# Attention and two feed-forward layers on one core: score, read and S matmuls of a batch gathered into two steps instead of three

## The chip, the cores and the metric

The kernel runs on one core of one Trainium2 chip. The metric is the device time of one execution in microseconds (us), from the profiler's clock; before the change three executions took 1313.85, 1314.18 and 1314.67 us.

## The reference, cut to what matters

For each of 8 batches and 8 heads an attention with 32 state rows is computed in both directions, and the joined output (4,608 tokens of 512 numbers) goes through two feed-forward layers with squared ReLU, 512 to 2,048 to 512.

```
scores = scale * x @ state.T ; a = softmax(scores) ; xread = a @ state
scores2 = scale * state @ x.T ; a2 = softmax(scores2) ; sread = a2 @ x
x = concat([xread, sread], axis=2) as (B * S, H * D)
h = max(x @ w_in, 0) ; x = (s * h * h + b) @ w_out          # first layer
h = max(x @ w_in2, 0) ; out = (h * h) @ w_out2              # second layer
```

## The kernel before, in words

Numbers are float32. Most matmuls run on a fast 32-bit format, with every operand split into a high and a low part (`hi`, `lo`), so that one product takes three matmuls.

**Steps.** The first layer is a loop over steps i. A step belongs to one batch j (512 tokens) and one block f of 128 hidden units, 16 steps for a batch. Batches 0 and 1 share steps 0 to 31, batch 2 has steps 32 to 47, batch 3 has 48 to 63, and so on; the last 16 steps are for the 256 state rows of all batches. A step issues 6 matmuls `h` (`mm1`), the ReLU, square and copy on ScalarE (ACT), a subtraction on VectorE (DVE, `low`), and the 12 matmuls `acc` (`mm2`) of the step two before. When a batch's 16 blocks are summed, `evac` takes the four accumulators out: two on DVE, two on ACT, into tiles `ot`, which are stored.

**What rides between the steps.** While batch j runs, the attention of batch b = j + 1 is made ready by jobs that `at_step(step, job, rank)` hangs on the steps. `base` is the first step of the batch that runs meanwhile. Those with matmuls are: `att_sc`, the scores `sc` (16 matmuls, copied out by ACT into the tile `sc`); `att_tp`, 8 transposes `tp` of the softmax (copied by ACT into `a2T`); `att_sr`, the reads `sr` (64 small matmuls), which `att_scale` multiplies on DVE; `att_put`, a transpose `st` of the scaled reads; and `s_mm` for each quarter q of the hidden units, which makes S, the product of the state and `w_in`. One S has 16 matmuls into two PSUM banks, two ACT copies (`S`, the high parts, in `s_parts`), and two DVE subtractions in `s_rest`, which read the same two banks again for the low parts. Scores and S use a quarter-width, half-height piece of the array (64*32 in the rows), reads 128*32, everything else the whole array.

**Order.** The program sets the order by hand; each engine runs its instructions in the order in which the jobs are called, by step and inside a step by rank. On ACT and DVE the same steps carry the preparation of the second layer's weights, one `sums_job` for each of 16 blocks with 15 operations: two loads, `magnitude` on ACT (tile `v`), `bound` and `shift`, `sign` and `low_bits` on DVE (two instructions each), four additions, four `hi` copies on ACT and four `lo` subtractions on DVE. The table `SUMS_AT` gives each operation its step; inside a step they have ranks 8 to 9, so they come behind the attention's jobs.

**Banks.** Every PSUM tile but the accumulators comes from `pst`, which takes four banks in turn (`psa`, `psb`, `psc`, `psc`). So the tile made four calls later sits in the same bank, and its first matmul waits until the last reader of the earlier tile is done.

**`behind`.** On a step listed in `behind`, the 12 `acc` matmuls of the following step are issued at once, behind the step's jobs, and only then the job itself, here `s_rest`:

```
for _, _, fn in sorted(side.pop(i, [])):
    fn()
if i in behind:
    rest_of(i - 1)
    behind.pop(i)()
```

Of the kernel before, what the change touches and what calls it, by code (L numbers as in the profile page):

```python
# [27 lines left out]
F32 = mybir.dt.float32  # L28
# [12 lines left out]
P = 128  # L41
# [47 lines left out]
def attn_mlp2(ctx: ExitStack, tc: tile.TileContext, xT, xn, st, w_in1, w_out1, w_in2, w_out2, s_in, b_in, out):  # L89
# [285 lines left out]
    def s_rest(b, q):  # L375
        t = S_t[b, q]
        for r in range(2):
            nc.vector.tensor_tensor(
                out=t[:, 1, r, :], in0=S_ps.pop((b, q, r)), in1=t[:, 0, r, :].bitcast(F32), op=ALU.subtract
            )  # L380
# [63 lines left out]
    xa = {}  # L444
    sb_t = {}

    def st_load(b):
        sb = sm.tile([P, 2, KD, NS], F32, tag="st", name=f"st{b}")
        nc.sync.dma_start(out=sb, in_=st[b])
        sb_t[b] = sb  # L450

    def att_load(b):
        t = x8([P, KD, S], f"xT{b}", F32)
        kk = KD // 2 if b < 2 else KD
        for k in range(0, KD, kk):
            nc.sync.dma_start(
                out=t[:, k : k + kk, :], in_=xT[b, k * P : (k + kk) * P].rearrange("(k p) s -> p k s", p=P)
            )
        xa[b] = [t, None]

    def att_load_n(b):
        n = x8([P, S // P, DM], f"xn{b}", F32)
        nc.sync.dma_start(out=n, in_=xn[b].rearrange("(t p) d -> p t d", p=P))
        xa[b][1] = n
# [132 lines left out]
    def att_scale(b):  # L597
        srp = srp_t.pop(b)
        s2 = parts2.pop(b)
        pool, tag = (an1, "an") if b else (op, "o")  # L600
        t = pool.tile([P, P], F32, tag=tag, name="srs").rearrange("p (r d) -> p r d", r=2)
        srp_t[b] = t
        for r in range(2):
            src, by = srp[:, r * D : (r + 1) * D], s2[:, r : r + 1]
            if b < 2:
                nc.scalar.activation(out=t[:, r], in_=src, func=ACTF.Copy, scale=by)
            else:
                nc.vector.tensor_scalar(out=t[:, r], in0=src, scalar1=by, scalar2=None, op0=ALU.mult)

    def att_put(b):  # L610
        t = srp_t.pop(b)
        pt = pst(f"st{b}")[:, :P]
        nc.tensor.transpose(out=pt, in_=t.rearrange("p r d -> p (r d)"), identity=ident)
        dst, src = sraw[:, :, b * NS : (b + 1) * NS], pt.rearrange("p (k n) -> p k n", k=KD)
        copy = lambda: nc.scalar.activation(out=dst, in_=src, func=ACTF.Copy)
        return copy if b == 0 else copy()
# [567 lines left out]
    def at_step(i, fn, rank=5):  # L1184

        side.setdefault(i, []).append((rank, len(side.get(i, ())), fn))
# [5 lines left out]
    def step(j, f):  # L1192
        return place[j, 0] + f

    calm = ((att_sc, 5, 0), (att_max, 6, 5), (att_exp, 8, 5), (att_sum, 9, 5), (att_mul, 10, 5), (att_tp, 13, 0),
            (att_sr, 17, 0), (att_scale, 17, 2))
    behind = {}
    for b in range(1, B):
        base = step(2, 0) + (b - 3) * NF if b > 1 else 0
        if b > 1:  # L1200
            at_step(base + 1 + (b == 2), lambda b=b: st_load(b), 6)
            at_step(base + 1, lambda b=b: att_load(b), 6)
            at_step(base + (4 if b > 2 else 1), lambda b=b: att_load_n(b), 6)
            for fn, k, r in calm:
                at_step(base + k, lambda fn=fn, b=b: fn(b), r)
            for c in range(2):
                n = base + 11 + c
                at_step(n, lambda b=b, c=c: att_turn(b, c), 3)
                at_step(n, lambda b=b, c=c: turned.pop((b, c))(), 6)
            at_step(base + (21 if b < B - 1 else 18), lambda b=b: att_put(b), -1)  # L1210
            if b == 2:
                for q in range(NQ):
                    k = base + 4 * q + 5
                    at_step(k, lambda b=b, q=q: s_mm(b, q), 1)
                    at_step(k + (q == 0), lambda b=b, q=q: s_rest(b, q), 0.2 if q == 0 else 9.8)
                continue
            for q, (k, r) in enumerate(((5, 1), (13, 1), (17, 1), (17, 2.5))):
                at_step(base + k, lambda b=b, q=q: s_mm(b, q), r)
            for q in range(2):
                at_step(base + 5 + 8 * q, lambda b=b, q=q: s_rest(b, q), 9.8)  # L1220
            behind[base + 17] = lambda b=b: s_rest(b, 2)
            at_step(base + 18, lambda b=b: s_rest(b, 3), 0.2)
            continue
        for q, n in ((1, 12), (2, 16), (3, 23)):
            at_step(n, lambda b=b, q=q: s_mm(b, q), 1)
            at_step(n + 1, lambda b=b, q=q: s_rest(b, q), 0.2)
# [338 lines left out]
```

## Time and profile before

| what | before |
|---|---|
| median of three executions | 1314.18 us (1313.85 to 1314.67) |
| the profiled execution | 1313.79 us, of which the span of instructions is 1312.0 us |
| TensorE (PE) busy | 1304.6 us, 99% of the span |
| PE weight loads, DVE, ACT busy | 1117.6, 921.6, 805.7 us |
| granted TensorE clock, mean | 1.000 of full speed |

The span runs from the first to the last instruction. PE is the engine that is always at work; the other engines have spare time, which costs nothing as long as PE needn't wait for them. Matmuls overlap, so the time that one costs is read from the start of one row to the start of the next, not from its own length.

### The profile page before, as it was taken

What the parts mean: (1) busy time and instruction counts of PE and PEld (TensorE: products, weight loads), DVE (VectorE), ACT (ScalarE), POOL (GpSimd) and SP (SyncE); (2) the same over time, 40 slices, a digit from 0 to 9 for tenths busy, and PEclk for the clock granted to TensorE, in tenths of its full rate; (3) what the DMA queues carried; (4) which work ended last, traced back from release to release, by engine and by line L of the source; (5) the groups of instructions that cost most, each with busy time, mean ns of one, the idle gap of its engine ahead of it and who ended that gap; (6) DMA issues with size and microseconds to landing.
All of it is one profiled execution on the core that took longest, in us unless ns stands there. A gap on an engine that the chain in (4) does not pass through costs nothing.

```text
span 1312.0 us, 21131 instructions
## 1 busy us (share of the span) xinstructions
PE 1304.6 (99%) x7455; PEld 1117.6 (85%) x7455; DVE 921.6 (70%) x1612; ACT 805.7 (61%) x1482; POOL 0.7 (0%) x7
## 2 busy tenths in 40 slices
PE   8999999999999999999999999999999999999998
PEld 6777777777787878789988888888899999999998
DVE  8998998676676767555456578666776776677665
ACT  6876756676666666766655465445554655565554
POOL 0000000000000000000000000000000000000000
PEclk9999999999999999999999999999999999999999
DMA  8467343443726273440576587665887798788775
GB/s 297 151 229 270 125 151 126 154 147 118 225 89 213 80 243 107 145 153 33 173 212 177 170 265 208 200 179 169 260 265 226 230 323 253 230 278 290 239 224 167
DMA packets 159560, 255.68 MB, mean 195 GB/s; under 512 B 14816, under 2 KB 67040, under 8 KB 159200
## 3 DMA queue, kind: packets, MB, share of 16 engines
q1 hardware_dynamic: 159456, 254.34, 61.3%
q8 instruction: 60, 0.98, 0.3%
q14 instruction: 44, 0.36, 0.1%
HBM read 202.90 MB, written 51.38 MB: 194 GB/s over the span
## 4 chain that ended last, share of the span: by engine, by line
PE 95%; DVE 4%; issue 0%; DMA 0%; ACT 0%; SPq 0%; DVEq 0%
PE acc L691 27%; PE m L923 25%; PE p L947 25%; PE h L642 14%; PE S L353 2%; PE sr L588 1%; PE sc L353 0%; DVE V L172 0%; DMA i1r<-w_in 0%; PE tp L574 0%; DVE g L674 0%; DVE v L172 0%; DVE V L179 0%; DVE o1l L227 0%; DVE V L158 0%
## 5 line engine op out<-in xcount | busy, mean ns | idle before, releaser
L923 PE MATMUL m<-bigx,bigr 128*128 128x384 f32 (+1 forms) x1680 | 366.9, 356 | 0.0
L691 PE MATMUL acc<-g,o1h 128*128 128x512 f32 (+1 forms) x1152 | 341.1, 378 | 0.1
L923 PEld LDWEIGHTS m<-bigx,bigr 128*128 128x128 f32 x1680 | 302.7, 188 | 26.4
L691 PEld LDWEIGHTS acc<-g,o1h 128*128 128x128 f32 x1152 | 211.8, 188 | 45.4 <-issue 3.4
L691 PE MATMUL acc<-g,o1l 128*128 128x512 f32 (+1 forms) x576 | 217.4, 378 | 0.0
L642 PE MATMUL h<-aT,S 128*128 128x512 f32 x768 | 196.9, 393 | 0.0
L947 PE MATMUL p<-g,bigr 128*128 128x384 f32 (+1 forms) x864 | 191.0, 356 | 0.0
L674 DVE TENSOR_TENSOR g<-r,g 128x512 fp32r<-128x512 f32 (+1 forms) x143 | 93.9, 657 | 132.5 <-ACT g L663 132.0
L642 PEld LDWEIGHTS h<-aT,S 128*128 128x128 f32 x768 | 142.2, 188 | 45.3 <-ACT a2T L575 5.0
L947 PEld LDWEIGHTS p<-g,bigr 128*128 128x128 f32 x864 | 155.9, 188 | 13.1
L657 ACT ACTIVATE r<-h 128x512 f32<-128x512 f32 (+1 forms) x143 | 81.7, 571 | 118.1 <-PE h L642 115.5
L750 ACT ACTIVATE sc<-sc 128x384 f32<-128x384 f32 (+1 forms) x120 | 67.9, 566 | 101.3 <-DVE sc L753 100.0
L947 PE MATMUL p<-bigg,bigr 128*128 128x384 f32 (+1 forms) x576 | 129.7, 357 | 0.0
L691 PEld LDWEIGHTS acc<-g,o1l 128*128 128x128 f32 x576 | 108.4, 188 | 20.2
L947 PEld LDWEIGHTS p<-bigg,bigr 128*128 128x128 f32 x576 | 104.1, 188 | 8.9
L750 ACT ACTIVATE v<-m 128x384 f32<-128x384 f32 (+1 forms) x80 | 42.8, 535 | 95.1 <-PE m L923 94.6
L753 DVE TENSOR_TENSOR v<-m,r 128x384 f32<-128x384 f32 (+1 forms) x40 | 24.5, 611 | 106.7 <-PE m L923 106.7
L660 ACT ACTIVATE r<-r 128x512 f32<-128x512 f32 (+1 forms) x143 | 87.1, 609 | 4.5
L663 ACT ACTIVATE g<-r 128x512 fp32r<-128x512 f32 (+1 forms) x143 | 87.0, 608 | 4.5
L753 DVE TENSOR_TENSOR g<-bigt,g 128x384 fp32r<-128x384 f32 (+1 forms) x71 | 41.9, 604 | 16.4 <-ACT g L750 16.3
L753 DVE TENSOR_TENSOR r<-m,v 128x384 f32<-128x384 f32 (+1 forms) x40 | 24.4, 611 | 35.0 <-PE m L923 31.8
L750 ACT ACTIVATE t<-t 128x384 f32<-128x384 f32 (+1 forms) x80 | 45.2, 565 | 1.3
(173 smaller groups left out, 1550.7 us busy)
## 6 DMA issues: line engine op xcount, KB each, us to landing
bigr<-wi SPq DMA_DIRECT2D x280, 256.0 KB, 3.2
bigr<-wo SPq DMA_DIRECT2D x240, 256.0 KB, 3.3
i1r<-w_in SPq DMA_DIRECT2D x16, 512.0 KB, 4.4
xn<-xn SPq DMA_DIRECT2D x8, 1024.0 KB, 9.2
o1r<-w_out SPq DMA_DIRECT2D x16, 512.0 KB, 5.4
x<-ot SPq DMA_DIRECT2D x32, 256.0 KB, 2.7
i2r<-w_in SPq DMA_DIRECT2D x32, 256.0 KB, 4.4
o2r<-w_out SPq DMA_DIRECT2D x16, 512.0 KB, 4.3
```

The costliest lines, as they stand in the source:

```text
L353: nc.tensor.matmul(out=outs[r][k * NS : (k + 1) * NS], lhsT=state[rows, r, k, :], rhs=moving(rows, k), start=True, stop=True, skip_group_c ...
L588: nc.tensor.matmul(out=srp[k * NS : (k + 1) * NS, r * D : (r + 1) * D], lhsT=a2Ts[r][:, i, k * NS : (k + 1) * NS], rhs=n[:, i, h * D : (h ...
L642: nc.tensor.matmul(out=hp, lhsT=l_, rhs=r_, start=(i == 0), stop=(i == len(ops) - 1))
L657: nc.scalar.activation(out=r, in_=hp, func=ACTF.Relu)
L660: nc.scalar.activation(out=r, in_=r, func=ACTF.Square)
L663: nc.scalar.activation(out=g[:, 0], in_=r, func=ACTF.Copy)
L674: nc.vector.tensor_tensor(out=g[:, 1], in0=r, in1=g[:, 0].bitcast(F32), op=ALU.subtract)
L691: nc.tensor.matmul(out=o, lhsT=l_, rhs=r_, start=(opens and i == 0), stop=(closes and i == 2))
L750: nc.scalar.activation(out=c, in_=src, func=func)
L753: nc.vector.tensor_tensor(out=out, in0=x, in1=y, op=op)
L923: nc.tensor.matmul(out=o, lhsT=w[:, a, k, :], rhs=x[:, b, k, :], start=(start and k + a + b == 0), stop=(k + a == 2), skip_group_check=True,)
L947: nc.tensor.matmul(out=o, lhsT=w[:, a], rhs=g[:, b], start=(opens and e == 0), stop=(u == NU - 1 and e == 2), skip_group_check=True,)
```

## The change

For batches 3 to 7 (b in the code) the jobs with matmuls stood on three steps of each 16: reads and two S on `base + 17`, the transpose `st`, scores and one S on `base + 5` (which is the 21st of the batch before), transposes and one S on `base + 13`. They now stand on two: scores on `base + 2`, where the reads and two S of the batch before also are (`base + 18` of that one), and `st`, transposes and two S on `base + 13`. Both steps use `behind`. The loads of x and of the state are issued three steps earlier, with the scores. The scaled reads are written over a piece of x's own tile (`xa`) instead of a tile of the pool `o`. Two operations of `SUMS_AT` are moved a step earlier: the second `sign` and `low_bits` of job 6 from step 67 to 66, the first of job 8 from 78 to 77. The number of instructions on each engine stays the same.

```diff
-    (64, 64, 66, 66, 66, 67, 67, 68, 68, 68, 68, 69, 69, 69, 70),
+    (64, 64, 66, 66, 66, 66, 67, 68, 68, 68, 68, 69, 69, 69, 70),
...
-    (75, 76, 78, 78, 78, 78, 79, 80, 79, 80, 80, 81, 80, 82, 82),
+    (75, 76, 77, 78, 78, 78, 79, 80, 79, 80, 80, 81, 80, 82, 82),
...
-        pool, tag = (an1, "an") if b else (op, "o")
-        t = pool.tile([P, P], F32, tag=tag, name="srs").rearrange("p (r d) -> p r d", r=2)
-        srp_t[b] = t
+        if b < 2:
+            pool, tag = (an1, "an") if b else (op, "o")
+            t = pool.tile([P, P], F32, tag=tag, name="srs")
+        else:
+            t = xa[b][1][:, 0, :P]
+        t = srp_t[b] = t.rearrange("p (r d) -> p r d", r=2)
...
-    calm = ((att_sc, 5, 0), (att_max, 6, 5), (att_exp, 8, 5), (att_sum, 9, 5), (att_mul, 10, 5), (att_tp, 13, 0),
-            (att_sr, 17, 0), (att_scale, 17, 2))
+    calm = ((att_max, 6, 5), (att_exp, 8, 5), (att_sum, 9, 5), (att_mul, 10, 5), (att_tp, 13, 0),
+            (att_sr, 18, 0), (att_scale, 18, 0.3))
...
-            at_step(base + 1 + (b == 2), lambda b=b: st_load(b), 6)
-            at_step(base + 1, lambda b=b: att_load(b), 6)
+            load = base + 1 if b == 2 else base - 2
+            at_step(load + (b == 2), lambda b=b: st_load(b), 6)
+            at_step(load, lambda b=b: att_load(b), 6)
             at_step(base + (4 if b > 2 else 1), lambda b=b: att_load_n(b), 6)
+            at_step(base + (5 if b == 2 else 2), lambda b=b: att_sc(b), -0.5)
...
-            at_step(base + (21 if b < B - 1 else 18), lambda b=b: att_put(b), -1)
+            at_step(base + (29 if b < B - 1 else 19), lambda b=b: att_put(b), -1)
...
-                    k = base + 4 * q + 5
+                    k = base + 4 * q + 5 + (q == 3)
...
-            for q, (k, r) in enumerate(((5, 1), (13, 1), (17, 1), (17, 2.5))):
+            for q, (k, r) in enumerate(((13, 1), (13, 2.5), (18, 1), (18, 2.5))):
                 at_step(base + k, lambda b=b, q=q: s_mm(b, q), r)
-            for q in range(2):
-                at_step(base + 5 + 8 * q, lambda b=b, q=q: s_rest(b, q), 9.8)
-            behind[base + 17] = lambda b=b: s_rest(b, 2)
-            at_step(base + 18, lambda b=b: s_rest(b, 3), 0.2)
+            for q in (0, 2):
+                k = base + (18 if q else 13)
+                behind[k] = lambda b=b, q=q: s_rest(b, q)
+                at_step(k + 1, lambda b=b, q=q: s_rest(b, q + 1), 0.2)
```

How the rows stand on the engines is shown at one place, around the reads of batch 4 (steps 65 and 66). DVE before, from the evacuation of batch 3 in step 65 on (`S_3356` and `S_3372` are the third and fourth S of batch 4):

```order
L719 TENSOR_SCALAR ot<-acc_2709,s_sb,cs 128x512
L608 TENSOR_SCALAR srs<-sr_3323,s_2909 128x64 x2
L674 TENSOR_TENSOR g<-r,g 128x512
L378 TENSOR_TENSOR S_3356<-S_3357,S_3356 128x512
L378 TENSOR_TENSOR S_3356<-S_3358,S_3356 128x512
L378 TENSOR_TENSOR S_3372<-S_3373,S_3372 128x512
L378 TENSOR_TENSOR S_3372<-S_3374,S_3372 128x512
L674 TENSOR_TENSOR g<-r,g 128x512
```

and DVE now, from the scaling of the reads in step 66 on (`S_3408` and `S_3421` are the same two S, and `i2r_3248` is the second half of job 6's weights):

```order
L611 TENSOR_SCALAR xn_2813<-sr_3373,s_2889 128x64 x2
L677 TENSOR_TENSOR g<-r,g 128x512
L172 SCALAR_TENSOR_TENSOR v<-i2r_3177,v 128x512
L179 SCALAR_TENSOR_TENSOR v<-i2r_3177,v 128x512
L158 TENSOR_SCALAR v<-v 128x512
L163 TENSOR_SCALAR v<-v 128x512
L172 SCALAR_TENSOR_TENSOR v<-i2r_3248,v 128x512
L179 SCALAR_TENSOR_TENSOR v<-i2r_3248,v 128x512
L378 TENSOR_TENSOR S_3408<-S_3409,S_3408 128x512
L378 TENSOR_TENSOR S_3408<-S_3410,S_3408 128x512
L378 TENSOR_TENSOR S_3421<-S_3422,S_3421 128x512
L378 TENSOR_TENSOR S_3421<-S_3423,S_3421 128x512
```

Between the reads' scaling and the low parts of S there are now `sign`, `low_bits` (L172, L179), `bound`, `shift` (L158, L163) and again `sign`, `low_bits`. ACT now, in the same step:

```order
L481 ACTIVATE sc<-sc_3360 128x512
L481 ACTIVATE sc<-sc_3361 128x512
L365 ACTIVATE S_3408<-S_3409 128x512
L365 ACTIVATE S_3408<-S_3410 128x512
L365 ACTIVATE S_3421<-S_3422 128x512
L365 ACTIVATE S_3421<-S_3423 128x512
L154 ACTIVATE v<-i2r_3248 128x512
```

The `magnitude` (L154) that fills the second `v` from `i2r_3248` comes behind the four copies of S. PE now, at the end of the same step and in the two after (`S_3422` and `S_3423` are the banks of the fourth S, `h_3457` and `h_3482` the hidden blocks of steps 67 and 68):

```order
L353 MATMUL S_3422<-V_1108,st_2517 32x512
L353 MATMUL S_3423<-V_1108,st_2517 32x512
L694 MATMUL acc_3344<-g,o1h_402 128x512 x2
L694 MATMUL acc_3344<-g,o1l_403 128x512
L694 MATMUL acc_3345<-g,o1h_402 128x512 x2
L694 MATMUL acc_3345<-g,o1l_403 128x512
L694 MATMUL acc_3346<-g,o1h_402 128x512 x2
L694 MATMUL acc_3346<-g,o1l_403 128x512
L694 MATMUL acc_3347<-g,o1h_402 128x512 x2
L694 MATMUL acc_3347<-g,o1l_403 128x512
L645 MATMUL h_3457<-aT_3051,S_3150 128x512 x6
L645 MATMUL h_3482<-aT_3051,S_3163 128x512 x6
```

The tile `h_3457` is the fourth call of `pst` behind `S_3409`, the first bank of the third S, and has the same bank. Steps 82 and 98 read the same way, with `bound`, `shift`, `sign`, `low_bits` of job 9 and with `bound`, `shift` of job 12 and four additions of job 11 ahead of the low parts of S, and a `magnitude` behind the copies of S on ACT. In steps 50 and 114 four additions stand there, and no `magnitude` on ACT that they wait for.

## Rows read from the trace of the kernel before

**Rows 1.** The page, section 1: busy time, share of the span, instructions.
```profile
PE 1304.6 (99%) x7455; PEld 1117.6 (85%) x7455; DVE 921.6 (70%) x1612; ACT 805.7 (61%) x1482; POOL 0.7 (0%) x7
```

**Rows 2.** Windows by stage: from:to, length, each engine's busy time, clock, DMA.
```profile
178.00:550.00 372.00, 372.00 (x2317) 291.81 (x2317) 259.35 (x454) 247.37 (x436) 0.00 (x0) 1.00 0.47 156
```

**Rows 3.** PE timeline, a step without jobs: start, length (us), line, tiles, count.
```profile
151.45 1.52 PE L642 MATMUL h<-aT,S 128*128 128x512 f32 x6
152.81 0.61 PE L691 MATMUL acc<-g,o1h 128*128 128x512 f32 x2
...
155.53 1.52 PE L642 MATMUL h<-aT,S 128*128 128x512 f32 x6
```

**Rows 4.** PE timeline, transposes and one S before batch 7.
```profile
523.39 1.03 PE L574 MATMUL tp<-ident,sc 128*128 128x128 f32 x8
524.36 1.09 PE L353 MATMUL S<-V,st 64*32 64x512 f32 x16
525.38 1.66 PE L642 MATMUL h<-aT,S 128*128 128x512 f32 x6
```

**Rows 5.** PE timeline, reads and two S of batch 6, step 97.
```profile
468.85 0.39 PE L691 MATMUL acc<-g,o1l 128*128 128x512 f32 x1
469.17 1.10 PE L588 MATMUL sr<-xn,a2T 128*32 128x64 f32 x64
470.20 1.95 PE L353 MATMUL S<-V,st 64*32 64x512 f32 x32
472.07 0.73 PE L691 MATMUL acc<-g,o1h 128*128 128x512 f32 x2
...
474.93 2.88 PE L642 MATMUL h<-aT,S 128*128 128x512 f32 x12
```

**Rows 6.** PE timeline, transpose, scores and one S, step 101.
```profile
488.53 0.27 PE L613 MATMUL st<-ident,srs 128*128 128x128 f32 x1
488.73 1.09 PE L353 MATMUL sc<-xT,st 64*32 64x512 f32 x16
489.62 1.06 PE L353 MATMUL S<-V,st 64*32 64x512 f32 x16
490.61 1.66 PE L642 MATMUL h<-aT,S 128*128 128x512 f32 x6
```

**Rows 7.** ACT timeline: S copies of step 97; job copies and magnitudes, steps 80 and 82.
```profile
471.38 2.06 ACT L365 ACTIVATE S<-S 128x512 fp32r<-128x512 f32 x4
...
391.55 1.13 ACT L289 ACTIVATE o2h<-v 128x512 fp32r<-128x512 f32 x2
...
405.56 1.21 ACT L154 ACTIVATE v<-o2r 128x512 f32<-128x512 f32 x2
```

**Rows 8.** DVE timeline, steps 82 and 83, idle time in brackets.
```profile
405.69 0.69 DVE L674 TENSOR_TENSOR g<-r,g 128x512 fp32r<-128x512 f32 x1 [3.95 <-ACT g L663]
406.30 0.68 DVE L293 TENSOR_TENSOR v<-v,o2h 128x512 fp32r<-128x512 f32 x1
407.23 0.42 DVE L158 TENSOR_SCALAR v<-v 128x512 f32<-128x512 f32 x1
407.69 0.43 DVE L163 TENSOR_SCALAR v<-v 128x512 uint32<-128x512 uint32 x1
408.15 0.69 DVE L172 SCALAR_TENSOR_TENSOR v<-o2r,v 128x512 uint32<-128x512 uint32 x1
408.88 0.69 DVE L179 SCALAR_TENSOR_TENSOR v<-o2r,v 128x512 uint32<-128x512 uint32 x1
```

**Rows 9.** Lines by form, 160 to 545 us: count, busy us, mean ns of one.
```profile
L378 DVE TENSOR_TENSOR S<-S,S 128x512 fp32r<-128x512 f32 x41 | 26.1, 685 | 15.3 <-ACT S L365 15.3
...
L278 DVE TENSOR_TENSOR v<-v 128x256 f32<-128x256 f32 x42 | 16.5, 421 | 0.5
```

**Rows 10.** ACT timeline, accumulators taken out of batch 2; first reads on PE behind.
```profile
252.56 0.69 ACT L717 ACTIVATE ot<-acc,s_sb 128x512 f32<-128x512 f32 x1 [2.62 <-DMA x<-ot]
...
250.05 1.10 PE L588 MATMUL sr<-xn,a2T 128*32 128x64 f32 x64
```

## The prediction

> **What bounds the kernel now.** I read the page's busy times first, then the windows by stage, then TensorE's timeline around each place where the jobs stand. TensorE is busy in 1304.6 of 1312.0 us [rows 1], and in the stretch that holds the changed steps it's busy in all 372.00 of 372.00 us, at full clock [rows 2]. So in the first layer nothing else ends a step: a step without jobs lasts 155.53 - 151.45 = 4.08 us, 1.36 for 6 `h` and 2.72 for 12 `acc`, 0.227 a matmul [rows 3]. Whatever a job costs TensorE there is added to the total, whatever another engine does is hidden, and the change can win only what the jobs cost beyond their matmuls. It can lose wherever TensorE must now wait; before, it waits nowhere in this stretch.
>
> **What is removed: breaks on TensorE.** The price of a group of jobs is the time that it puts between the whole-array matmuls, start to start.
>
> Reads and two S: the last `acc` starts at 468.85, the reads could follow at 469.08 and start at 469.17, so going over costs 0.09; then 1.03 for the reads, 1.87 for two S, and the 12 `acc` behind take 2.86 instead of 2.72, so coming back costs 0.14 [rows 5]. Sum 3.13. Transposes and one S: 0.97 + 1.02 [rows 4] + 0.14 = 2.13, without a cost of going over, since the transposes use the whole array. `st`, scores and one S: 0.20 + 0.89 + 0.99 [rows 6] + 0.14 = 2.22. A second S adds only 1.87 - 1.02 = 0.85.
>
> Gone are: reads and two S four times (batches 3 to 6), 12.52; reads and one S for batch 2, 0.09 + 1.03 + 1.02 + 0.14 = 2.28; `st`, scores and one S five times, 11.10; transposes and one S five times, 10.65. Together 36.55 us. In their place come: scores, reads and two S four times, each 0.09 + 1.02 + 1.03 + 1.87 + 0.14 = 4.15, where I let the scores cost what an S does that has no other S beside it; the same with one S for batch 2, 3.30; `st`, transposes and two S five times, each 0.12 (an eighth of the eight transposes) + 0.97 + 1.87 + 0.14 = 3.10. Together 16.60 + 3.30 + 15.50 = 35.40 us. The gain is 1.15 us, from five breaks fewer.
>
> No row shows the scores going over into the reads. If that were free, scores would cost 0.89, and the gain is 1.8; if it cost a full 0.14 + 0.09 more, the gain is nothing. I stay with 1.02, between the two, since an S that comes in from or goes out to another form always shows about that. The `st` ahead of transposes may cost up to 0.20 instead of 0.12, 0.4 in all.
>
> [...]
>
> **What is added: a queue in front of the low parts of S.** The two S of step 66 fill all four banks that `pst` deals out, and the hidden block of step 67 must have the first of them. That bank is free when DVE has made the low part of S from it. Before, DVE had only the reads' scaling and `low` ahead of that. Now the second set of `bound`, `shift`, `sign`, `low_bits` of the second layer's weights stands ahead, and it needs a `magnitude` that stands on ACT behind the four copies of S. So DVE can't begin it before both S are done and copied. From the start of the two S:
>
> - ACT's first copy starts 471.38 - 470.20 = 1.18 later [rows 5, 7], and four take 2.06, to 3.24 [rows 7].
> - Two `magnitude` take 1.21, so one about 0.6, to 3.84 [rows 7]. Handing over to DVE I put at 0.05, as an estimate, to 3.9.
> - `bound`, `shift` and `sign` take 408.88 - 407.23 = 1.65 [rows 8]; `low_bits`, 0.69 long, about 0.61, since starts are some 0.08 closer than the length (405.69, 406.30) [rows 8]. To 6.15.
> - One low part of S takes 0.685 [rows 9], and 0.05 to hand over to TensorE: 6.9.
> - TensorE wants the bank after both S and 12 `acc`, 1.87 + 2.86 = 4.73 [rows 5].
>
> TensorE waits 2.15 us, in step 67 and, with the same rows, in step 83. In step 98 `bound` and `shift` (0.92) and four additions of 0.42 [rows 9], about 1.55, stand there: 3.9 + 0.92 + 1.55 + 0.685 + 0.05 = 7.1, a wait of 2.35. Sum 6.65 us. All that hangs on ACT's and DVE's later rows shifts along, and nothing gives the time back, since TensorE has no idle time that could absorb it [rows 2]. Bounds: with no time for handing over and `magnitude` at 0.5, 2.0 less 0.05 each, about 6.0 in all; with 0.2 at each handing over, 7.6.
>
> The moved operation of job 6 (step 67 to 66) puts `sign` and `low_bits` into this queue, 1.34 of the 2.15 us of that step; the one of job 8 (78 to 77) stands in a step that waits for no `magnitude`. Why the others don't wait: in steps 50 and 114 the four additions follow `low` with operands that are ready, so the low part is done near 0.6 (scaled reads) + 0.6 + 1.6 + 0.7 = 3.5, before 4.73. In the `st` steps (45, 61, 77, 93, 109) the next hidden block wants the bank that this step's own hidden block and then the first S had, and from the end of this step's block TensorE has 2.72 + 2.96 + 2.86 = 8.5 us to do; the longest DVE queue, in step 77, is about 2.0 (three ACT rows before `low` can start) + 4.2. Step 34 has one S and no `behind`, and its bank is wanted a step later.
>
> Does a later DVE row overtake one that waits? In step 82 DVE sits idle for 3.95 us before `low` (405.69), though the `lo` behind it (406.30) had its operand since the ACT copies at 391.55 [rows 7, 8]. It doesn't. [...] By that the stall comes and the sum is a loss; were it otherwise, the sum would be the gain of 1.15 alone.
>
> **Smaller edits.** The loads of x and state keep four steps, some 16 us, before their first reader, as before; they only pass some stores on SP's queue. Scaled reads in x's own tile take no new instruction, and free a slot of the pool `o`; their cover is that x's tile isn't wanted until two steps later than they are read. Accumulators: the last one of batch 2 leaves ACT at 252.56 + 0.69 = 253.25, because a slot waited for a store, 3.3 us after TensorE's last `acc` (250.05 - 0.09) [rows 10]. Before, 2.9 us of reads and S stood in between; now only the next `h` and nine `acc`, 1.36 + 2.04 = 3.40. That is just enough, and the wait is put at 0, at most 0.3. In the `st` steps the second S needs both transposes copied: if a copy starts 0.7 behind and takes 0.55, the second ends at 1.8, where TensorE wants it at 0.97 + 0.85 = 1.82. I put 0, at most 0.2 five times.
>
> **The sum.** +6.65 - 1.15 = +5.5 us. On the profiled execution's own 1313.79 that is 1319.3; on the median of 1314.18, which lies 0.4 higher, 1319.7.
>
> **Rivals.** (A) Not slower: no low part of S comes late. One mechanism would do: if ACT's `magnitude` were done by the time that the copies of the first S are, 1.5 us earlier at most, and DVE's queue shrank by another 0.65, the low part would end by 4.73, the point from which it decides. Then only the breaks count: 1313.0. Against it stand the order of the rows on both engines and rows 7 and 8. (B) The thin margins break as well: `acc` waits for accumulators at the five ends of a batch, or the second S for the transposes; 0.3 to 0.6 at each of up to ten places, 1321.5 to 1324. Rows 10 speak for it, the freed slot of `o` against. [...]
>
> **How the numbers follow.** About 0.2% is what a measurement of this kernel can tell from no change, 2.6 us. Forecast 0.80; A 0.09; B 0.07; C 0.04. The forecast's own bounds: waits 6.0 to 7.6, gain 0 to 1.8, small waits 0 to 1.3, so +4.2 to +8.0 at the corners. I go down to +2.8, for the case that one of the three waits doesn't come, and stop at +8: 1317.0 to 1322.2. A and C lie outside. Slower is everything but A (0.90); A at -1.15 us is within 0.2%, and only its best end could be faster: same 0.09, faster 0.01.
>
> **What would show it.** Right: TensorE idle about 2.1 us ahead of the first `h` of steps 67, 83 and 99, released by a low part of S on DVE, and nowhere else; on DVE an idle time ahead of `bound`, released by `magnitude`; two steps with jobs in 16 instead of three, at 4.15 and 3.1 us. Wrong: no idle time there, or some at the first `acc` of a batch, at the second S, or at every step with two S, which would make the sum another one.

## The result, and the profile after

The changed kernel takes 1323.27 us (median of six, 1321.42 to 1323.90) where the kernel before, in the same runs, takes 1314.04 (1313.81 to 1314.67): 1.0065 times as long, with a 95% interval of 1.0055 to 1.0076. That is slower by 9.2 us. The forecast was +5.5, with 1322.2 as its upper end, so the sign was right and the time lies outside the range. The profiled execution took 1322.47 us, with a span of 1320.6, 8.6 above that of before.

Of eleven executions of the changed kernel (these six and five of a control), the mean granted clock of TensorE was 1.000 in six, which took 1321.40 to 1322.82 us, and 0.998 or 0.997 in five, which took 1323.72 to 1326.01.

Section 1 of the page, and a window of the same length as [rows 2] (from, to, length, busy time of PE, PE weight loads, DVE, ACT, POOL, granted clock, DMA share, GB/s):

```profile
PE 1306.1 (99%) x7455; PEld 1118.1 (85%) x7455; DVE 920.4 (70%) x1612; ACT 803.8 (61%) x1482; POOL 0.7 (0%) x7
```

```profile
192.00:564.00 372.00, 365.04 (x2202) 286.69 (x2201) 250.95 (x442) 241.88 (x429) 0.00 (x0) 1.00 0.45 147
```

The same number of instructions, but TensorE, which had no idle time in this stretch, now has 372.00 - 365.04 = 6.96 us. The waits of the same stretch (engine, line, tile, what it waited for: us, times, longest) say where:

```profile
PE h L645 <- DVE S L378: 5.7, 3, 1.9
PE acc L694 <- ACT ot L720: 1.3, 1, 1.3
```

The first line is the forecast's: three waits, each for a low part of S. The second was forecast as nothing. TensorE's timeline at step 98, which answers to [rows 5] (start, length, line, tiles, count, idle time before and its releaser):

```profile
479.42 1.09 PE L353 MATMUL sc<-xT,st 64*32 64x512 f32 x16
480.43 1.10 PE L588 MATMUL sr<-xn,a2T 128*32 128x64 f32 x64
481.46 1.95 PE L353 MATMUL S<-V,st 64*32 64x512 f32 x32
483.34 0.74 PE L694 MATMUL acc<-g,o1h 128*128 128x512 f32 x2
...
488.29 1.90 PE L645 MATMUL h<-aT,S 128*128 128x512 f32 x7 [1.89 <-DVE S L378]
```

From start to start the scores take 480.43 - 479.42 = 1.01, the reads 1.03, the two S 1.88: the prices that the sum used. The 12 `acc` and the wait take 488.29 - 483.34 = 4.95, where the `acc` alone took 2.86 [rows 5]. So the wait costs 2.09. At the other two places, steps 66 and 82, the same stretch takes 4.93.

What the wait is made of stands on DVE in step 82, beside two rows of ACT:

```profile
408.43 0.42 DVE L293 TENSOR_TENSOR o2h<-o2h 128x256 fp32r<-128x256 f32 x1
410.51 0.43 DVE L158 TENSOR_SCALAR v<-v 128x512 f32<-128x512 f32 x1 [1.67 <-ACT v L154]
410.98 0.43 DVE L163 TENSOR_SCALAR v<-v 128x512 uint32<-128x512 uint32 x1
411.44 0.69 DVE L172 SCALAR_TENSOR_TENSOR v<-o2r,v 128x512 uint32<-128x512 uint32 x1
412.17 0.69 DVE L179 SCALAR_TENSOR_TENSOR v<-o2r,v 128x512 uint32<-128x512 uint32 x1
412.77 2.48 DVE L378 TENSOR_TENSOR S<-S,S 128x512 fp32r<-128x512 f32 x4
```

```profile
407.88 2.06 ACT L365 ACTIVATE S<-S 128x512 fp32r<-128x512 f32 x4 [0.96 <-PE S L353]
409.80 1.24 ACT L154 ACTIVATE v<-o2r 128x512 f32<-128x512 f32 x2
```

ACT copies four pieces of S, then makes the `magnitude` (`v`). DVE idles 1.67 us for it, does `bound`, `shift`, `sign` and `low_bits`, and only then the low parts of S, the first of which ends near 413.5, where TensorE's `h` starts:

```profile
413.51 3.03 PE L645 MATMUL h<-aT,S 128*128 128x512 f32 x12 [1.88 <-DVE S L378]
```

The wait that wasn't forecast is in step 50, behind the end of batch 2. TensorE, then DVE and ACT, and last DVE before the change:

```profile
250.55 1.52 PE L645 MATMUL h<-aT,S 128*128 128x512 f32 x6
251.91 0.62 PE L694 MATMUL acc<-g,o1h 128*128 128x512 f32 x2
...
255.64 0.73 PE L694 MATMUL acc<-g,o1h 128*128 128x512 f32 x2 [1.30 <-ACT ot L720]
...
256.54 1.09 PE L353 MATMUL sc<-xT,st 64*32 64x512 f32 x16
```

```profile
244.15 0.69 DVE L677 TENSOR_TENSOR g<-r,g 128x512 fp32r<-128x512 f32 x1 [1.66 <-ACT g L666]
...
251.88 1.40 DVE L726 TENSOR_SCALAR ot<-acc,s_sb 128x512 f32<-128x512 f32 x2
```

```profile
240.34 1.66 ACT L289 ACTIVATE i2h<-v 128x512 fp32r<-128x512 f32 x3
...
242.21 0.57 ACT L660 ACTIVATE r<-h 128x512 f32<-128x512 f32 x1
...
254.90 0.69 ACT L720 ACTIVATE ot<-acc,s_sb 128x512 f32<-128x512 f32 x1 [4.37 <-DMA x<-ot]
```

```profile
241.23 0.69 DVE L674 TENSOR_TENSOR g<-r,g 128x512 fp32r<-128x512 f32 x1 [2.06 <-ACT g L663]
...
249.50 1.41 DVE L723 TENSOR_SCALAR ot<-acc,s_sb 128x512 f32<-128x512 f32 x2
```

The 12 `acc` and what they wait for last 4.63 us (251.91 to 256.54), where 12 `acc` with a break behind them last 2.81: 1.82 lost. ACT's second accumulator waits 4.37 us for a tile `ot` that a store has to free, and the store waits for DVE, which takes its two accumulators out at 251.88: the stores of these tiles are issued at 252.65. The last `acc` of the batch ended at 250.55 (the start of the next `h`), so DVE begins 1.33 us behind it. Before the change it began at 249.50, 0.46 us ahead of it (249.96, from [rows 10]). The `low` of step 47 (`g`) starts at 244.15 now, 6.40 us ahead of the batch's end, where it started 8.73 ahead of it. At the end of batch 6 the same stretch lasts 3.11, 0.30 lost.

**The account of the profile.** Three waits with a slower start behind them (12 `h` of 2.85 to 2.89 us instead of 2.72) 6.7; accumulators 1.82 and 0.30; fewer breaks -1.15. Together +7.67. Another 0.64 lies at 68 us, ahead of anything that the change touches (12 `acc` of 3.77 us, 3.13 before); in the profile of the control it is 0.21. The rest of 8.6 is spread in tenths. The median over the six executions with a clock of 1.000 is 1321.66 us, 7.6 above before: the account. The median of the first six, 1323.27, is the midpoint between the slowest at 1.000 (1322.82) and the fastest below it (1323.72), so the clock, below, has a part in it. Two of the six, 1322.47 and 1322.82, lie 0.8 and 1.2 above 1321.66 at a clock of 1.000; of the profiled one's 0.8, 0.43 stand at 68 us, where the control doesn't have them, and the rest isn't explained. Executions of e1 and e3, below, spread as far, by 1.5 and 1.7 us, all at 1.000.

### The profile page after: what moved, and what is told of

Read it like the earlier page. It is cut to its first block, busy times and chain, and to the rows that moved or that the text cites. A ratio compares the mean times of both kernels' runs of the same rounds, so it can differ in the third digit from the quotient of the medians.

```text
span 1320.6 us, 21139 instructions
## 1 busy us (share of the span) xinstructions
PE 1306.1 (99%) x7455; PEld 1118.1 (85%) x7455; DVE 920.4 (70%) x1612; ACT 803.8 (61%) x1482; POOL 0.7 (0%) x7
## 4 chain that ended last, share of the span: by engine, by line
PE 92%; ACT 2%; DVE 2%; DMA 2%; issue 1%; SPq 0%; ACTq 0%; DVEq 0%
PE acc L694 25%; PE p L950 25%; PE m L926 25%; PE h L645 14%; PE S L353 2%; DMA o1r<-w_out 1%; PE sr L588 1%; PE sc L353 0%; DMA i1r<-w_in 0%; ACT S L365 0%; PE tp L574 0%; DVE v L172 0%; ACT r L663 0%; ACT v L154 0%; ACT r L660 0%
```

## The experiments

All kernels but the first control are edits of the changed kernel; each was run between executions of the kernel before, whose median was 1314.04 to 1314.23.

**e0, the control.** No edit.

> The kernel after, unchanged, as a control in the same runs. Theory (three waits of 2.1 us, and behind each of them the granted clock may or may not fall to half, 1.55 us a time): runs at 1321.4 to 1322.8 with a mean clock of 1.000 and runs 1.5 to 3 us above them at 0.998 or 0.997; the profile has any fall of the clock right behind one of the three waits and nowhere else. Rival (the slower runs are slow from the start of the span, or all along): the clock falls elsewhere too, or the groups of 12 h behind the waits are of one length in all profiles.

Measured: 1321.40, 1321.64 and 1321.68 us at a clock of 1.000, 1324.76 and 1326.01 at 0.997. The profile was of one at 1.000, with a granted clock of 1.00 in the windows over the 12 `h` behind the three waits (338 to 342, 413 to 417 and 488 to 492 us), which last 2.85 to 2.86. That runs lie at levels, and which, is as expected. Neither profile of the changed kernel caught a fall of the clock, so where it falls is read from the near variants e2, e4 and e7.

**e1, low parts of S ahead of the jobs on DVE.**

```diff
-                behind[k] = lambda b=b, q=q: s_rest(b, q)
+                behind[k] = lambda: None
+                at_step(k, lambda b=b, q=q: s_rest(b, q), 7.5)
```

> The low parts of the two S stand ahead of the second layer's job operations on DVE in steps 50, 66, 82, 98 and 114; nothing else is changed from the kernel after. Theory (the queue of job operations ahead of the low parts makes TensorE wait): the first low part is then done about 0.6 + 0.6 + 1.2 us behind the start of the two S, before the 4.73 us at which TensorE wants the bank, so the three waits ahead of the first h of steps 67, 83 and 99 vanish, -6.7 us: about 1316.6 where the kernel after has 1323.3. The wait at the accumulators of step 50 (1.8 us) stays. Rival (two S beside each other fill the banks too long by themselves, through ACT's four copies): the waits stay at about 2 us each and the time at 1323. Rival (the clock falls behind a wait): also the 1.2 to 2.5 us go by which the slower half of the runs of the kernel after lies above its faster half, 1315 to 1316 in all runs.

Measured: 1314.87 us (1314.61 to 1316.11, eleven executions), 1.0008 of before (0.9999 to 1.0016), all at a clock of 1.000. DVE in step 82:

```profile
404.12 0.68 DVE L677 TENSOR_TENSOR g<-r,g 128x512 fp32r<-128x512 f32 x1
405.40 1.29 DVE L378 TENSOR_TENSOR S<-S,S 128x512 fp32r<-128x512 f32 x2 [0.60 <-ACT S L365]
406.60 0.68 DVE L293 TENSOR_TENSOR v<-v,o2h 128x512 fp32r<-128x512 f32 x1
```

The low parts follow the first copies at once and the jobs stand behind them. The 12 `acc` ahead of the three `h` last 2.89 us, as in e10, where no wait shows, so the waits are gone. The four banks and the two S together are therefore not what makes TensorE wait. Against the 1321.66 of the changed kernel at clock 1.000 this is -6.8, and no execution has a clock below 1.000, so the falls of the clock go with the waits. The 1.8 at step 50 stayed (4.60).

**e2, one pair of operations moved back.** The sixth entry in the row of job 6, its second `sign` and `low_bits`:

```diff
-    (64, 64, 66, 66, 66, 66, 67, 68, 68, 68, 68, 69, 69, 69, 70),
+    (64, 64, 66, 66, 66, 67, 67, 68, 68, 68, 68, 69, 69, 69, 70),
```

> Of the kernel after, only the second layer's sixth job is changed: the sign and low_bits that were moved from step 67 to 66 stand in step 67 again. Theory (every DVE operation ahead of the low part counts in full): the wait ahead of step 67's first h falls by the 1.34 us of these two, from 2.09 to about 0.75; the waits at 83 and 99 stay at 2.09; in all -1.3 us, about 1322.0. Rival (the wait is set by ACT's magnitude and its handing over, or by the copies of S): the wait at 67 stays near 2.1 and the time near 1323.3.

Measured: 1321.58 us (1319.93 to 1321.80): 1319.93 and 1320.16 at 1.000, three near 1321.7 at 0.999. TensorE in step 67:

```profile
336.57 3.02 PE L645 MATMUL h<-aT,S 128*128 128x512 f32 x12 [0.43 <-DVE S L378]
```

The stretch of 12 `acc` falls from 4.93 to 3.48, by 1.45 for operations of 1.34, and the other two keep their length (4.94, 4.95). So what stands in DVE's queue counts in full. The change's other moved operation, of job 8, stands in a step behind which no wait shows.

**e3, `magnitude` ahead of the copies on ACT.** DVE's order unchanged.

```diff
-            at_step(t, fn, 8 + (e == 6) / 2 + (7 <= e < 11) / 4)
+            early = e in (0, 3) and t in (66, 82, 98)
+            at_step(t, fn, -0.7 if early else 8 + (e == 6) / 2 + (7 <= e < 11) / 4)
```

> Of the kernel after, only ACT's order is changed: in steps 66, 82 and 98 the magnitudes of the second layer's weights stand ahead of the copies of the scores and of S; DVE's order is as in the kernel after. Theory (DVE's job operations are late because they wait for a magnitude that stands behind four copies): DVE's queue then runs without that wait and is done about 0.6 + 0.6 + 2.3 + 0.7 = 4.2 us behind the start of the two S where there is one set of bits, and about 5.5 where there are two (step 66), so that of 6.7 us of waits 0 to 1.5 are left: 1316.6 to 1318. Rival (the length of DVE's queue alone makes the wait, not what it waits for): the waits stay within 0.5 us of 2.1 each, and the time at 1322 to 1323.3. Rival (the copies of S are now the late ones, since the magnitudes of 0.6 us each are ahead of them): the low parts wait for ACT, and a wait of 0.5 to 1 us is left in step 83, where two magnitudes stand.

Measured: 1316.26 us (1315.99 to 1317.65), 1.0016 of before (1.0007 to 1.0025), a clock of 1.000 in all eleven. DVE in step 82, with no idle time ahead of `bound` (L158):

```profile
406.32 0.42 DVE L293 TENSOR_TENSOR o2h<-o2h 128x256 fp32r<-128x256 f32 x1
406.65 0.42 DVE L158 TENSOR_SCALAR v<-v 128x512 f32<-128x512 f32 x1
...
408.91 2.48 DVE L378 TENSOR_TENSOR S<-S,S 128x512 fp32r<-128x512 f32 x4
```

The `acc` stretches last 3.57, 3.18 and 2.90 us: 0.72, 0.33 and 0.05 left, where 2.07 to 2.09 were lost at each. With the same number of operations ahead of the low part, more than four fifths of the loss came from where `magnitude` stood on the other engine. The rest, 0.72 in step 67 and 0.33 in step 83, is the queue's length: DVE works without a pause there, in step 66 with two sets of bits. So the copies of S, behind two `magnitude` in step 82, are not what is waited for.

**e4, DVE freed ahead of batch 2's end.** One entry in the row of job 3, `sign` and `low_bits`.

```diff
-    (47, 47, 48, 48, 48, 48, 50, 51, 50, 51, 51, 52, 51, 52, 52),
+    (47, 47, 48, 48, 48, 50, 50, 51, 50, 51, 51, 52, 51, 52, 52),
```

> Of the kernel after, only one operation of the second layer's third job is moved, from step 48 to step 50, out of DVE's queue ahead of the evacuation of batch 2's last accumulators. Theory (the 1.8 us that TensorE waits at the accumulators of step 50 come from DVE, which begins its evacuation 1.3 us behind TensorE because of the job operations and the two low parts that the change put into steps 45 to 48): DVE begins the evacuation 0.7 to 1.4 us earlier, and the wait falls from 1.8 to 0.4 to 1.1 us; the three waits of 2.1 us stay; about 1322.3. Rival (the wait is set by the store that frees an output slot, whose start doesn't depend on DVE's queue): the wait stays at 1.8 us and the time at 1323.3.

Measured: 1321.50 us: 1320.43, 1321.37 and 1321.50 at 1.000, 1323.44 and 1323.67 at 0.997. At full clock the median is only 0.3 below that of the changed kernel, less than the spread between executions, so the repair is read from the trace, not from the time. DVE takes the accumulators out at 249.83, 0.13 ahead of the last `acc`'s end (249.96), and ACT's wait falls from 4.37 to 2.90:

```profile
252.84 0.69 ACT L720 ACTIVATE ot<-acc,s_sb 128x512 f32<-128x512 f32 x1 [2.90 <-DMA x<-ot]
```

The stretch at step 50 lasts 3.15, so 1.48 of 1.82 are gone, for 1.34 us of operations. The store isn't late by itself; it is late because DVE is. The profile was of an execution with a mean clock of 0.997, and shows where it fell. TensorE in steps 66 and 67, and windows of 1 us around it (the column behind POOL's is the granted clock):

```profile
334.67 0.39 PE L694 MATMUL acc<-g,o1l 128*128 128x512 f32 x1
336.93 4.61 PE L645 MATMUL h<-aT,S 128*128 128x512 f32 x12 [1.88 <-DVE S L378]
```

```profile
337.00:338.00 1.00, 1.00 (x5) 0.82 (x6) 1.00 (x3) 0.00 (x0) 0.00 (x0) 1.00 0.85 305
338.00:339.00 1.00, 1.00 (x4) 0.81 (x3) 0.67 (x2) 0.00 (x0) 0.00 (x0) 0.50 0.26 91
...
341.00:342.00 1.00, 1.00 (x5) 0.82 (x4) 1.00 (x2) 0.42 (x1) 0.00 (x0) 0.79 0.00 0
342.00:343.00 1.00, 1.00 (x7) 0.80 (x6) 0.97 (x3) 0.94 (x3) 0.00 (x0) 1.00 0.00 0
```

About 1 us after TensorE works again, the granted clock drops to 0.50 and stays there to 341.4. The 12 `h` take 341.34 - 336.93 = 4.41 us instead of 2.85 to 2.89: 1.5 us. In this profile it happens behind the waits of steps 67 and 99, not behind the one at 83; in e2's behind that of 83 and not of 99 (in windows of 10 us, e4's clock is 0.90 and 0.93 from 330 to 350, 1.00 from 410 to 420, 0.91 and 0.92 from 480 to 500; e2's is 0.83 from 410 to 420 and 1.00 in the other places).

**e12, step 45 without `behind`.** What made DVE late there? In the changed kernel the 12 `acc` come ahead of `h` of step 46, so two hidden blocks reach ACT one behind the other.

```diff
-                behind[k] = lambda b=b, q=q: s_rest(b, q)
+                if (b, q) == (3, 0):
+                    at_step(k, lambda b=b, q=q: s_rest(b, q), 7.5)
+                else:
+                    behind[k] = lambda b=b, q=q: s_rest(b, q)
```

> Of the kernel after, only step 45 (batch 3's transposes and first two S) no longer puts the next step's 12 acc ahead of its h; everything else as in the kernel after. In the kernel after, the 1.8 us wait at the accumulators of step 50 begins four steps earlier: with 12 acc first, the hidden block of step 46 starts 2.86 us later, two blocks reach ACT directly behind each other, low of step 47 on DVE comes 2.3 us later against the end of the batch than before the change, and DVE works without a pause from there to the evacuation. Theory (that order is the first cause): the evacuation is again early and the extra at step 50 falls from 1.82 to 0.3 at most; in return the h of step 46 now wants the first S's bank at once and waits for its low part, done 1.8 + 0.69 us behind the start of the two S, which last 1.88: about 0.6 us. In all about -1.0 to -1.2 us, 1320.5 to 1320.7 where the clock doesn't fall behind one of the three waits. Rival (the length of DVE's queue from the job operations alone decides): the extra stays at 1.2 us or more at step 50, and with the new wait the time is the same or longer.

Measured: 1320.22, 1320.30 and 1320.72 at 1.000 (median of all five 1320.72; the others 1322.03 and 1324.31). TensorE in step 46, DVE at the batch's end:

```profile
233.81 1.66 PE L645 MATMUL h<-aT,S 128*128 128x512 f32 x6 [0.61 <-DVE S L378]
```

```profile
249.81 1.41 DVE L726 TENSOR_SCALAR ot<-acc,s_sb 128x512 f32<-128x512 f32 x2
```

DVE begins to take the accumulators out 0.45 us ahead of the last `acc`'s end (250.26), as before the change, and the stretch at step 50 lasts 2.84: 0.03 lost instead of 1.82. The same jobs are in DVE's queue. The edit also puts the first low part of step 45 ahead of the jobs on DVE, but e1 has that too, with the 12 `acc` still ahead of `h`, and there the stretch lasts 4.60. So the order at step 45 on TensorE is the first cause. The queue's length hands it on: e4, which shortened the queue and kept the order, took most of it back as well.

**e7, a longer wait.** Two more sets in the row of job 9.

```diff
-    (82, 82, 82, 82, 83, 83, 84, 86, 85, 87, 87, 87, 86, 88, 89),
+    (82, 82, 82, 82, 82, 82, 84, 86, 85, 87, 87, 87, 86, 88, 89),
```

> Of the kernel after, only two sets of operations of the second layer's ninth job are moved from step 83 to 82, where they stand on DVE ahead of the low part of S: bound and shift (0.92 us) and sign and low_bits (1.34 us). Theory (every DVE operation ahead of the low part counts in full): the wait ahead of the first h of step 83 grows from 2.09 by 2.26 to about 4.35 us, the waits at 67 and 99 stay; about 1325.5 without a fall of the clock. Rival (other queues limit it): less than half of that. On the clock: in two profiles the granted clock stood at half for about 3.5 us behind a wait of 2.1 us, which made the next 12 h 1.55 us longer, and in others of the same kernel it didn't. If the length of the wait decides, it falls behind this one of 4.35 us in every run, and no run is below 1326.5; if it is chance, the runs lie apart as before, from 1324.

Measured: 1326.61 us (1325.42, 1325.88, 1327.34, 1327.41). TensorE and the clock in step 83:

```profile
414.99 4.61 PE L645 MATMUL h<-aT,S 128*128 128x512 f32 x12 [4.14 <-DVE S L378]
```

```profile
415.00:416.00 1.00, 1.00 (x3) 0.85 (x4) 1.00 (x2) 0.00 (x0) 0.00 (x0) 0.71 1.03 422
416.00:417.00 1.00, 1.00 (x4) 0.72 (x4) 0.72 (x2) 0.00 (x0) 0.00 (x0) 0.50 0.78 320
```

The `acc` stretch lasts 7.20, 4.35 more than 2.85: 2.26 us of operations lengthen the wait by 2.26. The clock falls to 0.50 behind this wait. The span of the profile, 1324.1, is 4.3 us above e0's 1319.8; the longer wait and one fall, 12 `h` of 4.45 instead of 2.86, make 3.85, and a second fall would make 5.4, so this is nearer to one fall than to two. All four executions are below 1.000 and at least 1.5 us above the 1323.9 that the sum gives at full clock (1321.66 + 2.26), which is one fall or more. The bound that I had set, none below 1326.5, was missed by two; it had started from 1325.5 at full clock, which is too high. Only the profiled execution shows a fall behind this wait; in the other three it could be one of the shorter two. That a wait of this length always brings the fall is not shown.

**e6, both repairs.** The low parts as in e1, and two jobs' operations moved behind the ends of batches 2 and 6.

```diff
-    (47, 47, 48, 48, 48, 48, 50, 51, 50, 51, 51, 52, 51, 52, 52),
+    (47, 47, 48, 48, 50, 50, 50, 51, 50, 51, 51, 52, 51, 52, 52),
-    (111, 111, 112, 112, 112, 112, 114, 115, 114, 115, 115, 116, 115, 116, 116),
+    (111, 111, 112, 112, 114, 114, 114, 115, 114, 115, 115, 116, 115, 116, 116),
```

> The kernel with the low parts of S first, and besides of the third and of the second to last job of the second layer the second bound and shift and the second sign and low_bits each two steps later (48 to 50, 112 to 114), behind the evacuation of a batch's last accumulators instead of ahead of it. Theory (three waits for S, waits for accumulators at two batch ends and nothing else eat the gain of 1.15 us): the extra 1.79 us of the 12 acc behind step 49 and the 0.28 us behind step 113 go as well, so about 1314.87 - 2.1 = 1312.8, that is 1.2 us below the kernel before: the gain of the breaks shows at last. Rival (the store that frees the output slot is late for another reason): the extra stays at 0.4 us or more at step 50, 1313.2 to 1313.7. Rival (the breaks don't give 1.15 us): 1314 or more with no wait in the trace.

Measured: 1314.49 us (1314.18 to 1315.46), 1.7 above the forecast. Both ends of a batch are free (2.81), but there is a wait in step 116 that wasn't there:

```profile
553.87 1.65 PE L645 MATMUL h<-aT,S 128*128 128x512 f32 x6 [1.22 <-DVE S L378]
```

What I moved to step 114 stands there ahead of the second S's low part. I had made the change's own mistake again, one queue further on.

**e10, that pair in step 113 instead.**

```diff
-    (111, 111, 112, 112, 114, 114, 114, 115, 114, 115, 115, 116, 115, 116, 116),
+    (111, 111, 112, 112, 113, 113, 114, 115, 114, 115, 115, 116, 115, 116, 116),
```

> The kernel e6, in which moving two operations of the second to last job from step 112 to 114 had put them ahead of the second low part of S there (a wait of 1.22 us ahead of the first h of step 116, with its restart 1.34); now they stand in step 113, behind the evacuation. Theory: that wait goes and no other comes, so 1314.49 - 1.34 = 1313.15, 0.9 us below the kernel before; the groups between the whole-array matmuls take 4.15 and 3.1 us as in the kernel after. Rival (moved again: the evacuation's outputs or the scaled reads of step 114 come late instead): 1314 or more, with a wait in steps 113 to 117.

Measured: 1313.10 us (1312.68 to 1313.79, eleven executions, all at 1.000), before 1314.23 (1313.68 to 1315.65): ratio 0.9991, 0.9982 to 1.0000. From 100 to 600 us TensorE waits for nothing. TensorE in step 83, with no wait ahead of `h`:

```profile
404.13 0.74 PE L694 MATMUL acc<-g,o1h 128*128 128x512 f32 x2
...
407.02 2.88 PE L645 MATMUL h<-aT,S 128*128 128x512 f32 x12
```

This is the only version below the kernel before. Its 1.1 us would be the 1.15 of the breaks, but the interval reaches to 1, and 0.1% is less than what a measurement here can tell from no change. The profiles show the stretch itself. From the `h` of step 33 to the first `h` of the state rows, a stretch that holds all the moved matmuls, TensorE before and in e10:

```profile
173.97 1.52 PE L642 MATMUL h<-aT,S 128*128 128x512 f32 x6
...
602.25 0.40 PE L642 MATMUL h<-xsr,i1h 128*128 128x256 f32 x2
```

```profile
174.29 1.52 PE L645 MATMUL h<-aT,S 128*128 128x512 f32 x6
...
601.57 0.40 PE L645 MATMUL h<-xsr,i1h 128*128 128x256 f32 x2
```

That is 428.28 us before and 427.28 in e10, 1.00 us less, in one profile of each.

**e11, one break more in five places.** The second S by itself, a step later, in e10.

```diff
-            for q, (k, r) in enumerate(((13, 1), (13, 2.5), (18, 1), (18, 2.5))):
+            for q, (k, r) in enumerate(((13, 1), (14, 1), (18, 1), (18, 2.5))):
-                at_step(k + 1, lambda b=b, q=q: s_rest(b, q + 1), 0.2)
+                at_step(k + 2 - q // 2, lambda b=b, q=q: s_rest(b, q + 1), 0.2)
```

> The kernel e10 with the second S of each group with the transposes one step later, alone: one more break in five places, nothing else. Theory (a break has a fixed price: 0.09 to go over, 0.14 to come back, and an S by itself 1.02 instead of the 0.85 that it costs behind another S): + 0.40 us in five places, 2.0 us above e10, about 1315.2. Rival (the breaks as such cost nothing measurable, and the gain of the change is only an accident of the waits): the same time as e10.

Measured: 1315.23 us (1314.70 to 1316.72), 2.1 above e10, and no wait between 100 and 600 us. The S by itself:

```profile
455.06 1.52 PE L645 MATMUL h<-aT,S 128*128 128x512 f32 x6
456.51 1.09 PE L353 MATMUL S<-V,st 64*32 64x512 f32 x16
457.53 1.65 PE L645 MATMUL h<-aT,S 128*128 128x512 f32 x6
```

6 `h` take 1.36, so going over costs 0.09, the S 1.02, and coming back 0.13 or 0.15. The price of a break holds, and shows in the whole time.

**e9, scores apart, in e6.**

```diff
-            at_step(base + (5 if b == 2 else 2), lambda b=b: att_sc(b), -0.5)
+            at_step(base + (5 if b == 2 else 3), lambda b=b: att_sc(b), -0.5)
```

> The kernel e6 with the scores of batches 3 to 7 taken out of the group with the reads and two S, one step later, alone: one more break on TensorE in five places. Theory (a break costs 0.09 us to go over and 0.13 us to come back, and scores by themselves 0.89 to 1.02 us): each of the five groups of scores then costs 1.12 to 1.25 us instead of the 1.02 by which it made the group longer, so 0.5 to 1.15 us in all above e6. Rival (scores beside reads were the dearer form): nothing or a gain against e6.

Measured: 1319.96 us (1319.81 to 1321.11), 5.5 above e6 instead of 0.5 to 1.15. It says nothing on the break: a step later the scores themselves want a bank whose low part isn't made yet, and the five groups of scores last 1.54 to 2.42 us, together 4.5 more than at 1.02 each. The waits name it in one place:

```profile
PE sc L353 <- DVE S L378: 0.4, 1, 0.4
```

## Why the forecast was right and wrong

**The breaks: right.** The groups cost 4.15 us (0.09 + 1.02 + 1.03 + 1.88 + 0.13) and 3.10 (0.11 + 0.97 + 1.88 + 0.14), where the sum had 4.15 and 3.10. e10 shows the gain by itself, 1.00 us in the profiles for 1.15, and e11 the price, 2.1 for 2.0. In the runs a break costs about 0.23 us: 0.09 to go over and 0.13 or 0.15 to come back, in e11.

**The three waits: right, their sum partly by luck.** Forecast 2.15, 2.15 and 2.35, measured 2.07, 2.07 and 2.09: 6.23 for 6.65. The slower start behind them, 0.13 to 0.17 each and 0.45 in all, was not in the sum; that 6.7 meets 6.65 so closely is two errors that cancel. Steps 67 and 83 came out as derived. In step 98 the queue was worked out as 0.2 longer than it is. For each handing over the sum had 0.05, a guess for which no row of the trace before stood; in step 82 of the changed kernel `bound` starts 410.51 - 409.80 = 0.71 behind a `magnitude` of 0.68 to 0.69, and `h` 413.51 - 412.77 = 0.74 behind a low part of 0.685, so it took 0.02 to 0.03 and 0.06. e1 and e3 show the two halves of the cause: the place of the low part behind the jobs on DVE, and that of `magnitude` behind the copies on ACT. That a row on DVE doesn't overtake one that waits is right too. In step 82 of the changed kernel all four pieces of S were copied at 409.94, and DVE began their low parts at 412.77, behind the rows that had waited.

**The accumulators: the first step that failed.** "That is just enough, and the wait is put at 0, at most 0.3" was wrong by 1.82 us in step 50, and right at batch 6's end (0.30). I took the time at which ACT was done from [rows 10] as if it stayed where it was against TensorE. But the change puts `behind` on step 45. That shifts the next hidden block by 12 `acc`, two blocks reach ACT together, `low` of step 47 comes 2.3 us later, and DVE has nothing left to catch up with before the batch ends. e12 against e1 shows this cause, e4 the queue that hands it on. Rival B had the place, with a price of 0.3 to 0.6 at up to ten places; it was 1.82 at one and 0.30 at another. That the measured time lies in B's range of 1321.5 to 1324 is not B's doing alone: without the clock it would be at its lower end.

**The clock: the second step that failed, a term put at nothing.** The sum has no term for the clock. A fall of the clock behind the same waits was the case C, beside the forecast and outside its range, with a chance of 0.04; the trace before, with a clock of 1.00 in [rows 2], shows no fall. In the runs it does come on top of the forecast's waits, 1.55 us a time, and only behind some of them. The mean clocks say that five of eleven executions of the changed kernel had at least one, and the profiles of e2 and e4 have each fall right behind a wait for a low part, as e7's has the one in step 83. This term, not the accumulators, takes the median out of the range: with the accumulators in it, the sum is 5.5 + 1.82 + 0.30 = 7.6, or 1321.8 at full clock, which is still below the 1322.2 at which the range ends. (Two executions at a clock of 1.000 lie above 1322.2, within the spread named above.) One fall gives 1323.3. That this is the measured 1323.27 is luck, since no execution took that time. In the windows of 1 us that lie wholly inside a fall the clock is 0.50, in those wholly outside 1.00; why the same wait brings the fall in one execution and not in the next, no run shows.

**The range: a sum that was wrong.** Its corners, worked out from its own bounds, are 6.0 - 1.8 = 4.2 and 7.6 + 1.3 = 8.9, not 8.0. Its upper end would have been 1323.1, still just below the median, so this is not what failed.

**Left open.** Whether a wait of 4.1 us always brings the fall, and why the same wait brings it in one execution and not in the next. The spread of up to 1.7 us between executions at full clock. And 0.64 us near 68 us in one profile, ahead of the change, is not explained.

## What to carry to other kernels

An instruction that is put ahead of another on an engine that runs its rows in order, as DVE did here (in step 82 the low parts began 2.83 us after their copies were done), costs what it waits for as well as what it takes, so write down for each moved wait which row on the other engine releases it and what stands ahead of that row; here a reordering on either engine took back most of the 6.7 us. When a step changes the order of the bottleneck's own work (here `acc` ahead of `h`), follow the shifted blocks through every engine to the next point with a thin margin, instead of taking that margin from the trace before. And where a forecast makes the bottleneck wait by some microseconds, a fall of its clock, here about 1.5 us behind some waits of 1.9 us, belongs in the sum with a chance, not among the rivals.

## What the runs showed of the hardware that I had not expected

Where TensorE had been busy at full clock for over 50 us, some waits of 1.9 us (e2, e4) were followed by a granted clock of 0.50, as was the one of 4.1 us in e7: from 0.1 to 1.1 us after it worked again and for about 3.4 us, worked out from the windows of three profiles (4.41 to 4.45 us for 12 `h` instead of 2.85 to 2.89). Such a fall comes in some executions of the same program and not in others (a mean clock of 0.997 or 0.998 in five of the changed kernel's eleven, 1.000 in six). Kernels whose profile shows no wait of more than 1.3 us in this stretch were never below a mean of 0.999 in 60 executions (e1, e3, e6, e9, e10, e11); all 33 of e1, e3 and e10 were at 1.000, and three of the others at 0.999. A mean of 0.999 alone is no sign of such a fall, since 6 of the kernel before's own 66 executions beside these runs, without any wait in this stretch of its profile, show it too. And behind its three waits of 1.9 us the changed kernel's first 12 `h` take 2.85 to 2.89 us, 0.13 to 0.17 more than 2.72, even at full clock.
